# Layer 1's last two token blocks as a seven-product pair, in a kernel of chunked attention and two feed-forward layers

## The chip, the cores and the metric

One core of a Trainium2 chip. The metric is the device time of one execution in microseconds (us), lower is better. The engines are TensorE (PE; its weight loads are listed as PEld), VectorE (DVE), ScalarE (ACT), GpSimd (POOL) and SyncE (SP, which issues all DMAs of this kernel). Each engine works through its own instructions in the order in which the program issues them.

## The reference

```
scores = scale * q_c @ k_c^T            # 8 batches, 8 heads, 9 chunks of 64 tokens, head size 64
attn   = softmax(scores)
x      = attn @ v_c                     # as 4608 tokens x 512
x      = gelu_sigmoid(x @ w_in1) @ w_out1      # 512 -> 2048 -> 512
out    = prelu(x @ w_in2, alpha) @ w_out2      # 512 -> 2048 -> 512
```

Activations are fp32; the weights arrive as 64-bit floats and are decoded on the chip. Each operand of a feed-forward product is split into a high part, which TensorE's fp32r format holds, and the rest, and a product is the sum of three passes: high by high, low by high, high by low.

## The kernel before

Tokens go in 36 groups of 128 (`NG`), four to a block of 512 (`NB`, 9 blocks). The kernel has two stages.

**Stage 1** computes layer 1 block by block. A slot n is one block j and one of its 16 slices f of the hidden size: `emit_h` issues 12 matmuls for h = x w_in (three passes by four row tiles), Gelu on ACT, a copy to the high part on ACT and a subtraction for the low part on DVE (helper `split`, L123); `emit_y` issues 12 matmuls of y += g w_out, two slots behind: slot n issues h(n), then y(n-2). At the ends of a block this changes: slice 15 issues y(n-2) and y(n-1), slice 0 issues the last y of the block before, and slice 1 issues none. There are 144 slots. The sums y of a finished block are copied from PSUM and stored to DRAM (`x2d`). Slice 15 also splits the next block's x (`split_x`).

The attention of the groups and the preparation of layer 2's weights are put between these matmuls by a plan of half slots: half slot 2n is what `middle()` issues after h(n), and 2n+1 what follows y(n-2). A group g has these steps: `att_T` (q and k transposed by DVE, in blocks of 32), `att_S` (scores on PE, a row maximum and a subtraction on DVE: `att_S_max`), `att_X` (exponential on ACT, which loads another table first), `att_N` (three DVE instructions for the inverse of the row sum, then one multiplication on POOL), `att_AT` (eight DVE transposes), `att_PV` (32 matmuls, followed by the 32 score matmuls of the next group, then two ACT copies). From group 4 on a group starts every eight half slots (L1015): T at -5, X at -1, N at 0, AT at 2, PV at 5, the next group's S matmuls and maximum with PV. q and k are loaded by `load_qk` (L304): 32 DMAs of 16 KB for a group, in runs of 128 bytes, already in the order that `att_T` wants.

Layer 2 uses a scheme of seven products (Strassen-Winograd) for pairs of token blocks, so stage 1 also prepares the weights' combinations, in 32 steps (L1005), one per 3.25 slots from slot 18: load, absolute value on ACT, decode on DVE (four instructions), `prep_store_a` (ACT copy, POOL subtraction, four POOL sums) and `prep_store_b` (the same without sums). High and low parts go to DRAM (`wi2`, `wo2`). The store of a part is issued at once, and SP waits for it.

**Stage 2** (`second_layer`) works through five pairs (`PAIRS`, twice 512, 512, 512, 384, 384 tokens). A pair has four weight groups; a weight group is 14 h items of 6 matmuls and 7 y items of 12. A clock counts 1 for each h item and 2 for each y item. After an h pair ACT and DVE gather the product (`h_after`), apply the PReLU (`below`: three ACT instructions, `join`: one on DVE), and split the y operands (`op_hi` on ACT, `op_lo` on DVE); POOL forms four differences (L801). Weight tiles come from DRAM through two rings, reloaded after each use. While the last block of stage 1 runs, the first pair's x is loaded (`x_load`), its four sums formed on POOL (`x_sums`) and its seven operands split (`x_hi`, `x_lo`).

Of the kernel before, what the change touches and what calls it, by code (L numbers as in the profile page):

```python
# [32 lines left out]
PREP_FROM = 18  # L33
PREP_EVERY = 3.25

PAIRS = (512, 512, 512, 384, 384)
# [6 lines left out]
PLACE = {1: 0, 2: 1, 3: 6, 4: 2, 5: 3, 6: 4, 7: 5}  # L43

# [6 lines left out]
def tile_chunk_attention_two_ffn(  # L51
# [23 lines left out]
    NG = NT // P  # L75
    HP = H // 2
# [8 lines left out]
    gt_p = ctx.enter_context(tc.tile_pool(name="gt", bufs=2))  # L85
# [3 lines left out]

    first = ExitStack()  # L90
# [4 lines left out]
    prep_p = first.enter_context(tc.tile_pool(name="prep", bufs=1, reuse_waits="tile"))  # L95
# [12 lines left out]

    wi2 = [dram.tile([P, 7, 2, 2, P], F32, name=f"wi2_{j}") for j in range(NF // 2)]
# [114 lines left out]
    def prep_store(step, lo, hi, t):  # L224
        kind, j, m = step
        dst = wi2[j][:, lo:hi, m] if kind == "wi" else wo2[j // 2][:, lo:hi, j % 2, m]
        nc.sync.dma_start(
            out=dst.rearrange("p i a f -> p i (a f)"),
            in_=t.bitcast(F32).rearrange("p i a f -> p i (a f)"),
        )  # L230
# [11 lines left out]
    def prep_split(src, n, tag):  # L242
        t = prep_p.tile([P, n, 2, P], F32R, tag=tag, name=tag)
        nc.scalar.copy(t[:, :, 0], src)  # L244
        nc.gpsimd.tensor_tensor(out=t[:, :, 1], in0=src, in1=t[:, :, 0].bitcast(F32), op=ALU.subtract)  # L245
        return t

    def prep_store_a(step):
        u = pr[step]
        prep_store(step, 0, 3, prep_split(u[:, 0:3], 3, "sta"))  # L250
        sums = dec_p.tile([P, 4, P], F32, tag="u", name="sums")
        a11, a12, a22, a21 = (u[:, q] for q in range(4))
        for o, x, y, op in (
            (0, a21, a22, ALU.add), (1, sums[:, 0], a11, ALU.subtract),
            (2, a11, a21, ALU.subtract), (3, a12, sums[:, 1], ALU.subtract),
        ):
# [65 lines left out]

    qkT = {}

    def att_T(g):

        for nm in ("q", "k"):
            a = qkv.pop((g, nm))
            if g < GPB:
                t = spare(f"wo{NF - 3 - g % 2}", nm == "k").rearrange("p (h t) -> p h t", h=HP)  # L330
            else:
                t = qkt_p.tile([P, HP, P], F32, tag=nm + "T", name=nm + "T")
            if g < GPB + 2:
                ps = psum_att("psT")
                for hp in range(HP):
# [129 lines left out]
    def att_PV(g):  # L465
        at, vt = at_t.pop(g), qkv.pop((g, "v"))
        blk, i = divmod(g, GPB)
        if i == 0:
            x_t[blk] = x_p.tile([P, KT, NB], F32, tag="x", name="x")
# [27 lines left out]
    def split_x(j):  # L497
        if j not in x_t:
# [18 lines left out]
    gs_t = {}  # L517

    def emit_h(n, middle):
# [12 lines left out]
        g = gs[:, 0] if whole else gt_p.tile([P, NB], F32, tag="g", name="g")  # L532
        if f == NF - 1:
            split_x(j + 1)
        nc.scalar.activation(out=g, in_=ps, func=AF.Gelu_apprx_sigmoid)  # L535
        middle()
        if not whole:
            split(g, gs[:, 0], gs[:, 1], nc.scalar, nc.vector)
# [4 lines left out]
    def emit_y(n):  # L543
# [10 lines left out]
        if f == NF - 1:  # L554
            for t, ps in enumerate(y_t.pop(j)):
                if j == NBLK - 1:
                    sb = wpool.tile([P, 512], F32, tag=f"wo{8 + t}", name="ysb")
                else:
                    sb = dec_p.tile([P, 512], F32, tag="u", name="ysb")
# [10 lines left out]
    starts = [2 * sum(PAIRS[:p]) for p in range(NP)]  # L570
# [16 lines left out]
    def second_homes():  # L587
# [3 lines left out]
        for nm in ("b21", "b22", "t1", "t2", "t4"):  # L591
            homes[nm] = sec_p.tile([P, 1024], F32, tag=nm, name="x_" + nm)
        homes["wi2"] = []
        for k in range(2):
            t = sec_p.tile([P, 2, 2, 2, P], F32R, tag=f"wi2_{k}", name="wi2t")
            homes["wi2"] += [t[:, 0], t[:, 1]]
        for _ in range(4):
            load_wi()
# [20 lines left out]
    def x_load(p):  # L619
        n, t0 = PAIRS[p], starts[p]  # L620
        for half in range(2):
            for done, step, blk, s in x2_pieces(t0 + half * n, n):
                for c, names in ((0, ("b11", "b12")), (2, ("b21", "b22"))):
                    nc.sync.dma_start(
                        out=wide(homes[names[half]], n)[:, :, done:done + step],
                        in_=x2d[blk][:, c:c + 2, s:s + step],
# [44 lines left out]

    def load_wi():
        if wi_order:
# [4 lines left out]
            nc.sync.dma_start(out=t.bitcast(F32), in_=wi2[2 * gr + jj][:, PLACE[i]])  # L678
            wi_q.append(t)

    def load_wo():
        if wo_order:
# [4 lines left out]
            nc.sync.dma_start(out=t.bitcast(F32), in_=wo2[gr][:, PLACE[i]])  # L687
            wo_q.append(t)

    def second_layer():  # L690
# [12 lines left out]
        op_homes = [(home(f"op{k}h", F32R), home(f"op{k}l", F32R)) for k in range(4)]  # L703
# [7 lines left out]
        def at(when, fn, *args):  # L711
            due.setdefault(when, []).append((fn, args))

# [44 lines left out]
        def h_after(p, gr, i, jj):  # L758
# [6 lines left out]
            if jj == 0:  # L765
                return
            if i == 4:
# [7 lines left out]
            else:  # L775
# [3 lines left out]
                def rest():  # L779
                    neg = next_neg(n)  # L780
# [93 lines left out]
        def y_out(p, q):  # L874
# [3 lines left out]
            t = wide(homes[("b21", "b22", "t1", "t2")[q]], n)  # L878
            for d in range(2):
# [35 lines left out]
        while hs or ys:  # L915

            def y_next():
                nonlocal clock
                clock += 2
                if slot == nh or slot > nh + 1:  # L920
                    item = ys.pop(0)
                    y_item(*item)
                    load_wo()
                    y_after(*item)
# [7 lines left out]
            for _ in range(2 if hs else 0):  # L932
# [7 lines left out]
                load_wi()  # L940
                h_after(*item)
# [8 lines left out]
    with tc.manual_schedule():  # L950
# [53 lines left out]
        ]  # L1004
        for i, step in enumerate(steps):  # L1005
            n = PREP_FROM + int(i * PREP_EVERY)
            for what, lag, fn in (
                ("prep", 1, prep_load), ("abs", 3, prep_abs), ("prep", 3, prep_decode),
                ("prep", 4, prep_store_a), ("prep", 5, prep_store_b),
            ):  # L1010
                todo.setdefault((what, n + lag), []).append(partial(fn, step))


        between = {}
        for g in range(GPB, NG):  # L1015
            for at, fn in zip((-5, -1, 0, 2, 5), (att_T, att_X, att_N, att_AT, att_PV)):
                if g > GPB or at > 0:
                    when = 8 * (g - GPB) + at
                    between.setdefault(max(4, when) if fn is att_T else when, []).append((fn, g))
            if g + 1 < NG:  # L1020
                between.setdefault(8 * (g - GPB) + 6, []).append((load_v, g + 1))
            if g + 2 < NG:
                for part in range(8):
                    between.setdefault(max(0, 8 * (g - GPB) - 1 + part), []).append(
                        (partial(load_qk, part), g + 2)
                    )
# [3 lines left out]
        last_att = max(between) // 2  # L1030
        for n in range(NBLK * NF):
# [3 lines left out]

            def middle():
                nonlocal dec
                for fn, g in between.get(2 * n, []):
                    fn(g)
# [9 lines left out]
            for fn in todo.get(("abs", n), []):  # L1049
                fn()  # L1050


# [4 lines left out]
            for fn, g in between.get(2 * n + 1, []):  # L1057
                fn(g)
            for key in todo.get(("load", n), []):
                load_w(*key)  # L1060
            for fn in todo.get(("prep", n), []):
                fn()
            if n == NBLK * NF - NF + 2:
# [3 lines left out]
                second_homes()  # L1067
                x_load(0)
                for fn in x_sums(0):
                    fn()  # L1070
            if n >= NBLK * NF - 12 and n % 2 == 0:
                i = H_ORDER[(n - (NBLK * NF - 12)) // 2] if n < NBLK * NF - 0 else None
                x_hi(0, i)
                x_lo(0, i)
            if n == NBLK * NF - NF + 7:
                wo2_homes()
            if n == NBLK * NF - 3:
                more_homes()
        x_hi(0, H_ORDER[6])
        x_lo(0, H_ORDER[6])  # L1080
        emit_y(NBLK * NF - 1)
        banks.close()
        second_layer()


# [28 lines left out]
```

## Time and profile before

| | us |
|---|---|
| three runs | 1588.76, 1592.19, 3175.36 |
| their median | 1592.19 |
| the profiled execution | 1587.85 |
| its span on the core | 1586.0 |
| PE busy | 1560.1 (98%) |
| DVE, ACT, POOL busy | 1070.3, 835.8, 439.6 |

The span runs from the first to the last instruction on the core; the execution has 1.85 us around it. A busy PE is not PE at its peak, since matmuls are pipelined: the pace is read from how far apart runs of matmuls start.

### The profile page before, as it was taken

The page shows a single profiled execution, that of the slowest core. Times are in us where ns is not written, and L with a number is a line of the kernel's source. Part 1 is how long each engine was busy: PE and PEld are TensorE (multiplying, and loading weights), DVE is VectorE, ACT ScalarE, POOL GpSimd, SP SyncE. Part 2 cuts the span into 40 slices and gives each one's busy share as a digit, 9 for nine tenths or more (in the row PEclk, how much of TensorE's full clock was granted, in tenths as well). Part 3 has the DMA queues.
Part 4 walks back from the last instruction along what each step waited for, and adds up shares of the span by engine and source line. Part 5 has one row for each costly group of instructions (what it writes and reads, how often), then busy time and mean ns, then how long its engine had stood idle before and what let it go on. Part 6 is the DMA issues. An engine that isn't in the chain of part 4 may idle for free.

```text
span 1586.0 us, 25307 instructions
## 1 busy us (share of the span) xinstructions
PE 1560.1 (98%) x9309; PEld 1310.0 (83%) x9312; DVE 1070.3 (67%) x1442; ACT 835.8 (53%) x1198; POOL 439.6 (28%) x343
## 2 busy tenths in 40 slices
PE   7999999999999999999999999999999999999997
PEld 5678888888888888888888788888888888999997
DVE  6897656575666666566332477876887788688766
ACT  4665554454445545444333555665666556546653
POOL 3001322222222232222120235223422343352320
PEclk9999999999999999999999999999999999999999
DMA  9662445544444545444150676689668866997974
GB/s 247 189 170 59 95 106 145 122 130 115 128 114 115 133 124 135 123 116 116 37 199 1 184 226 214 188 216 280 192 191 218 267 187 213 243 335 233 279 256 120
DMA packets 384044, 268.08 MB, mean 169 GB/s; under 512 B 264112, under 2 KB 321968, under 8 KB 383920
## 3 DMA queue, kind: packets, MB, share of 16 engines
q1 hardware_dynamic: 383920, 266.46, 59.6%
q8 instruction: 74, 1.21, 0.3%
q14 instruction: 50, 0.41, 0.1%
HBM read 218.11 MB, written 48.23 MB: 168 GB/s over the span
## 4 chain that ended last, share of the span: by engine, by line
PE 93%; DVE 4%; ACT 2%; issue 1%; DMA 0%; DVEq 0%; ACTq 0%
PE psY L550 25%; PE psH L526 25%; PE psHa L731 12%; PE psYa L849 12%; PE psYb L849 9%; PE psHb L731 9%; PE psX L477 1%; PE psX L388 1%; DVE o L796 1%; ACT neg L748 0%; ACT neg L746 0%; DVE g L777 0%; DVE yacc L867 0%; DVE u L170 0%; PE warm L966 0%
## 5 line engine op out<-in xcount | busy, mean ns | idle before, releaser
L526 PE MATMUL psH<-xs,wi 128*128 128x512 f32 x1728 | 421.5, 394 | 1.1 <-ACT gs L535 1.1
L550 PE MATMUL psY<-gs,wo 128*128 128x512 f32 x1644 | 393.6, 389 | 0.0
L526 PEld LDWEIGHTS psH<-xs,wi 128*128 128x128 f32 x1728 | 322.9, 188 | 71.5 <-ACT gs L535 1.4
L550 PEld LDWEIGHTS psY<-gs,wo 128*128 128x128 f32 x1644 | 308.3, 188 | 64.1
L535 ACT ACTIVATE g<-psH 128x512 f32<-128x512 f32 x137 | 82.0, 599 | 307.1 <-PE psH L526 298.3
L128 DVE TENSOR_TENSOR gs<-g,gs 128x512 fp32r<-128x512 f32 x137 | 104.8, 765 | 202.3 <-ACT gs L125 201.9
L849 PE MATMUL psYa<-o,w 128*128 128x512 f32 (+1 forms) x960 | 212.0, 368 | 4.0 <-DVE o L796 2.1
L731 PE MATMUL psHa<-xop,wi2t 128*128 128x512 f32 (+1 forms) x960 | 211.1, 368 | 1.8 <-ACT g L769 1.4
L849 PEld LDWEIGHTS psYa<-o,w 128*128 128x128 f32 x960 | 175.0, 188 | 28.3 <-DVE o L796 3.8
L731 PEld LDWEIGHTS psHa<-xop,wi2t 128*128 128x128 f32 x960 | 175.3, 188 | 25.8 <-ACT g L769 1.8
L849 PE MATMUL psYb<-o,w 128*128 128x512 f32 (+1 forms) x720 | 158.4, 368 | 0.7 <-ACT o L791 0.7
L731 PE MATMUL psHb<-xop,wi2t 128*128 128x512 f32 (+1 forms) x720 | 158.1, 368 | 0.0
L849 PEld LDWEIGHTS psYb<-o,w 128*128 128x128 f32 x720 | 131.3, 188 | 18.4 <-ACT o L791 1.3
L746 ACT ACTIVATE neg<-g 128x1024 f32<-128x1024 f32 (+1 forms) x80 | 78.2, 977 | 128.9 <-DVE g L777 128.3
L801 POOL TENSOR_TENSOR tsum<-g,tsum 128x1024 f32<-128x1024 f32 (+1 forms) x39 | 100.7, 2583 | 163.2 <-DVE o L796 163.2
L731 PEld LDWEIGHTS psHb<-xop,wi2t 128*128 128x128 f32 x720 | 131.5, 188 | 17.4
L801 POOL TENSOR_TENSOR tsum<-g,g 128x1024 f32<-128x1024 f32 (+1 forms) x19 | 42.0, 2209 | 341.8 <-DVE g L754 341.8
L754 DVE SCALAR_TENSOR_TENSOR g<-g,neg 128x1024 f32<-128x1024 f32 (+1 forms) x80 | 104.4, 1305 | 15.8 <-ACT neg L748 15.8
L245 POOL TENSOR_TENSOR sta<-u,sta 128x384 fp32r<-128x384 f32 x32 | 33.4, 1045 | 259.8 <-ACT sta L244 229.6
L796 DVE TENSOR_TENSOR o<-tsum,o 128x1024 fp32r<-128x1024 f32 (+1 forms) x60 | 69.1, 1151 | 49.7 <-ACT o L791 49.6
L748 ACT ACTIVATE neg<-neg,minus_alpha 128x512 f32<-128x512 f32 (+1 forms) x160 | 100.4, 675 | 2.6
L796 DVE TENSOR_TENSOR o<-g,o 128x1024 fp32r<-128x1024 f32 (+1 forms) x60 | 96.9, 1614 | 4.9 <-ACT o L791 4.9
(131 smaller groups left out, 1796.7 us busy)
## 6 DMA issues: line engine op xcount, KB each, us to landing
wi2t<-wi SPq DMA_DIRECT2D x280, 256.0 KB, 3.7
w<-wo SPq DMA_DIRECT2D x140, 512.0 KB, 3.8
x<-ysb SPq DMA_DIRECT2D x36, 256.0 KB, 2.6
raw<-in_moe_w_in_dram SPq DMA_DIRECT2D x16, 512.0 KB, 5.0
raw<-in_moe_w_out_dram SPq DMA_DIRECT2D x16, 512.0 KB, 4.0
raw<-in_moe_w_in_dram SPq DMA_DIRECT2D x32, 256.0 KB, 4.0
wi<-stb SPq DMA_DIRECT2D x16, 512.0 KB, 3.3
raw<-in_moe_w_out_dram SPq DMA_DIRECT2D x32, 256.0 KB, 3.6
```

The source lines that it names most:

```text
L128: eng_lo.tensor_tensor(out=lo, in0=src, in1=hi.bitcast(F32), op=ALU.subtract)
L245: nc.gpsimd.tensor_tensor(out=t[:, :, 1], in0=src, in1=t[:, :, 0].bitcast(F32), op=ALU.subtract)
L526: nc.tensor.matmul(ps, w[:, a, c], xs[:, b, c], start=(i == 0), stop=(i == 3 * KT - 1))
L535: nc.scalar.activation(out=g, in_=ps, func=AF.Gelu_apprx_sigmoid)
L550: nc.tensor.matmul(y_t[j][t], w[:, a, t * P:(t + 1) * P], gs[:, b], start=(f == 0 and a + b == 0), stop=(f == NF - 1 and b == 1),)
L731: nc.tensor.matmul(ps, w[:, c, a], x[b][:, c], start=(k == 0 and i in (1, 2, 5)), stop=(k == 5 and i in (2, 3, 4)), skip_group_check=True,)
L746: nc.scalar.activation(out=neg, in_=src, func=AF.Relu, scale=-1.0)
L748: nc.scalar.activation(out=neg[:, jj], in_=neg[:, jj], func=AF.Copy, scale=minus_alpha[:, f + jj:f + jj + 1])
L754: nc.vector.scalar_tensor_tensor(out=g, in0=g, scalar=0.0, in1=neg, op0=ALU.max, op1=ALU.add)
L796: nc.vector.tensor_tensor(out=lo, in0=wide(homes[nm], n), in1=hi.bitcast(F32), op=ALU.subtract)
L801: eng.tensor_tensor(out=wide(homes[out], n), in0=wide(homes[x], n), in1=wide(homes[y], n), op=ALU.subtract,)
L849: nc.tensor.matmul(ps[:, d, :n], w[:, jj, d, a], x[b][:, jj], start=(k == 0 and i in (1, 5, 2)), stop=(k == 5 and i in (3, 2, 4)), skip_gr ...
```

## The change

The last two blocks (7 and 8, groups 28 to 35) leave stage 1's slots, of which 112 are left (`NPL` = 7 blocks), and become a first pair of stage 2 (`PAIRS_1`) with layer 1's weights. Their attention output goes to DRAM (`x1d`). The pair has the same items as layer 2's, with Gelu where those have the PReLU, and its output goes to `x2d` without a transpose. Its weight combinations are made by a new POOL step `fold`, 32 times, one per 4.7 half slots from half slot 40: two additions of 128x256 (the high and low part of decoded weights) and four of 128x128; they are stored as fp32, and each weight tile is split when it has been loaded (`split_factor`: ACT copy; subtraction on POOL for w_in tiles of 128x256, on DVE for w_out tiles of 128x512).

All 32 groups must be done within 112 slots. From the fifth on they follow at six half slots, in the order `GROUP_ORDER`, the i-th at half slot base = 32 + 6(i-4). q and k of groups from 8 on are first copied from DRAM to DRAM (`sort_qk`, eight DMAs of 512 runs of 128 bytes for a group), then loaded as two whole tiles (`load_sorted`); `att_T` then writes every fourth column. The preparation's step i has b = 36 + int(5.5 i): load at half slot b, absolute value b+3, decode b+4, store_a b+6, store_b b+8. Within a half slot the plan lists attention first, then preparation and fold in the order of i. Stores of prepared tiles are issued two half slots later (`send_later`). The high part of g is copied before `middle()` instead of after it, from block 1 on. The diff, cut to its core:

```diff
-PREP_FROM = 18
-PREP_EVERY = 3.25
-PAIRS = (512, 512, 512, 384, 384)
+PREP_FROM = 36
+PREP_EVERY = 5.5
+FOLD_FROM = 40
+FOLD_EVERY = 4.7
+PAIRS_1 = (512,)
+PAIRS_2 = (512, 512, 512, 384, 384)
+PAIRS = PAIRS_1 + PAIRS_2
+GROUP_ORDER = (
+    4, 5, 6, 7, 8, 9, 10, 11, 28, 29, 12, 13, 14, 15, 30, 16, 17, 18, 19, 31,
+    20, 21, 22, 23, 32, 33, 24, 25, 26, 27, 34, 35,
+)
...
     def prep_store_a(step):
+        a11, a12, a22, a21 = (pr[step][:, q] for q in range(4))
+        sums = dec_p.tile([P, 4, P], F32, tag="u", name="sums")
+        quarter_sums(a11, a12, a21, a22, *(sums[:, o] for o in range(4)))
+        prep_store(step, 0, 3, prep_split(pr[step][:, 0:3], 3, "sta"))
...
+    def fold(step):
+        kind, j, m = step
+        u = prep_p.tile([P, 7, P], F32, tag="fold", name="fold")
+        for k in range(2):
...
+            nc.gpsimd.tensor_tensor(out=o, in0=t[:, 0], in1=t[:, 1], op=ALU.add)
+        a11, a12, a21, a22, s0, s1, s2 = (u[:, o] for o in range(7))
+        quarter_sums(a11, a12, a21, a22, s0, s1, s2, a21)
...
+    def sort_qk(part, g):
...
+            nc.sync.dma_start(
+                out=qk_d[g, nm][part % 4, off:off + n],
+                in_=src[b, par::2, s:s + n, y * SQ:(y + 1) * SQ].rearrange("h t e -> t h e"),
+            )
...
+            else:
+                nc.vector.transpose(
+                    t.rearrange("p h (t b) -> p b h t", b=4),
+                    a.rearrange("p (b h e) -> p b h e", b=4, h=HP),
                 )
...
         nc.scalar.activation(out=g, in_=ps, func=AF.Gelu_apprx_sigmoid)
+        early_hi = j > 0
+        if early_hi:
+            nc.scalar.copy(gs[:, 0], g)
         middle()
...
+    def split_factor(hi, lo, eng):
+        nc.scalar.copy(hi, lo.bitcast(F32))
+        eng.tensor_tensor(out=lo, in0=lo.bitcast(F32), in1=hi.bitcast(F32), op=ALU.subtract)
...
+        def split_soon():
+            while unsplit:
+                at(clock + 3, split_factor, *unsplit.pop(0))
...
+            if i == 4 and p < N1:
+                nc.scalar.activation(out=g("21"), in_=src, func=AF.Gelu_apprx_sigmoid)
+                return
...
+                    if p < N1:
+                        nc.scalar.activation(out=g(nm), in_=g(nm), func=AF.Gelu_apprx_sigmoid)
+                        return
...
-        for g in range(GPB, NG):
-            for at, fn in zip((-5, -1, 0, 2, 5), (att_T, att_X, att_N, att_AT, att_PV)):
+        for i, g in enumerate(GROUP_ORDER):
+            if i < GPB:
+                times = ((att_T, -5), (att_X, -1), (att_N, 0), (att_AT, 2), (att_PV, 5))
+            else:
+                times = ((att_T, -5), (att_S_max, -1), (att_X, 0), (att_N, 1), (att_AT, 2), (att_PV, 4))
...
-        for n in range(NBLK * NF):
+        for n in range(NPL * NF):
```

## Rows read from the trace of the kernel before

**Rows 1.** The page: busy shares (part 1), and PE's granted clock in slices (part 2).
```profile
PE 1560.1 (98%) x9309; PEld 1310.0 (83%) x9312; DVE 1070.3 (67%) x1442; ACT 835.8 (53%) x1198; POOL 439.6 (28%) x343
...
PEclk9999999999999999999999999999999999999999
```

**Rows 2.** Waits of PE: engine line, what it waited for; us, times, longest.
```profile
PE psS L359 <- ACT early L341: 2.5, 3, 1.1
PE psYa L849 <- DVE o L796: 2.1, 3, 1.1
```

**Rows 3.** By stretch: us, busy PE, PEld, DVE, ACT, POOL, PEclk, DMA, GB/s.
```profile
370.00:490.00 120.00, 120.00 (x822) 98.65 (x821) 73.27 (x134) 56.73 (x90) 32.18 (x42) 1.00 0.48 121
...
1027.50:1180.20 152.70, 152.70 (x674) 126.16 (x673) 120.49 (x99) 90.84 (x104) 55.62 (x21) 1.00 0.76 220
```

**Rows 4.** Chain that ended last, in order of time: start, us, piece (452 to 473 us).
```profile
452.77 0.62 PE psX L477 x32
...
459.54 2.72 PE psH L526 x12
...
464.98 2.72 PE psH L526 x12
```

**Rows 5.** Timeline of one group's attention steps in stage 1: start us, us, engine, line.
```profile
456.85 0.60 ACT L535 ACTIVATE g<-psH 128x512 f32<-128x512 f32 x1 [1.86 <-PE psH L526]
...
458.13 1.28 ACT L408 ACT_TABLE_LOAD   x1
...
459.42 0.63 ACT L408 ACTIVATE e<-e 128x512 f32<-128x512 f32 x1
...
460.09 0.69 DVE L413 TENSOR_REDUCE d<-e 128x8 f32<-128x512 f32 x1 [1.25 <-ACT e L408]
...
460.64 1.31 POOL L245 TENSOR_TENSOR stb<-sums,stb 128x512 fp32r<-128x512 f32 x1 [2.75 <-ACT stb L244]
...
460.81 1.18 DVE L414 TENSOR_SCALAR d<-d 128x8 f32<-128x8 f32 x1
...
462.30 1.04 POOL L416 TENSOR_TENSOR e<-e,d 128x512 f32<-128x512 f32 x1 [0.34 <-DVE d L415]
...
464.19 3.60 DVE L448 STREAM_TRANSPOSE at<-e 32x256 f32<-32x256 f32 x8
...
464.68 6.03 SPq L318 DMA_DIRECT2D q<-in_q_dram  x12
...
475.78 0.69 PE L477 MATMUL psX<-at,v 64*64 64x64 f32 x32
```

**Rows 6.** One line's instructions, duration ns min/median/max: the addition in `att_N`.
```profile
L414 DVE TENSOR_SCALAR d<-d x36: 171/174/1175, 11.7 to 761.0; 128x8 f32<-128x8 f32 x36
```

**Rows 7.** Groups by shape: instructions and operation, tiles, count | busy us, mean ns.
```profile
L343 DVE STREAM_TRANSPOSE qT<-q 128x512 f32<-128x512 f32 x30 | 21.1, 703 | 0.0
...
L170 DVE SCALAR_TENSOR_TENSOR u<-raw,u 128x512 int32<-128x512 int32 x64 | 43.0, 689 | 1.3
...
L160 DVE TENSOR_SCALAR u<-u 128x512 f32<-128x512 f32 x64 | 28.0, 455 | 3.6 <-ACT u L157 3.6
...
L245 POOL TENSOR_TENSOR sta<-u,sta 128x384 fp32r<-128x384 f32 x32 | 33.4, 1045 | 259.8 <-ACT sta L244 229.6 <-DMA k<-in_k_dram 30.1
...
L257 POOL TENSOR_TENSOR sums<-u,sums 128x128 f32<-128x128 f32 x32 | 15.2, 476 | 0.0
...
L128 DVE TENSOR_TENSOR gs<-g,gs 128x512 fp32r<-128x512 f32 x137 | 104.8, 765 | 202.3 <-ACT gs L125 201.9
```

**Rows 8.** Groups by shape, ACT and DVE instructions that the pair's steps use.
```profile
L746 ACT ACTIVATE neg<-g 128x1024 f32<-128x1024 f32 x48 | 51.0, 1063 | 82.2 <-DVE g L777 81.8
...
L748 ACT ACTIVATE neg<-neg,minus_alpha 128x512 f32<-128x512 f32 x96 | 64.4, 718 | 1.6
...
L487 ACT COPY x<-psX 128x256 f32<-128x256 f32 x72 | 23.2, 376 | 68.1 <-PE psX L388 63.4 <-PE psX L477 4.6
...
L754 DVE SCALAR_TENSOR_TENSOR g<-g,neg 128x1024 f32<-128x1024 f32 x48 | 72.4, 1508 | 12.3 <-ACT neg L748 12.3
```

More of the change, by code (lines that the diff above doesn't have):

```diff
@@ L106, in tile_chunk_attention_two_ffn @@
     x2d = [dram.tile([P, KT, NB], F32, name=f"x2_{j}") for j in range(NBLK)]
+    x1d = {j: dram.tile([P, KT, NB], F32, name=f"x1_{j}") for j in range(NPL, NBLK)}
+    wi1 = [dram.tile([P, 7, 2, P], F32, name=f"wi1_{j}") for j in range(NF // 2)]
+    wo1 = [dram.tile([P, 7, 2, 2, P], F32, name=f"wo1_{g}") for g in range(NF // 4)]
     wi2 = [dram.tile([P, 7, 2, 2, P], F32, name=f"wi2_{j}") for j in range(NF // 2)]
@@ L222, in prep_load, with send_later, send_due, prep_store @@
         pr[step] = decode_raw([raw.rearrange("p q f -> p (q f)")])
-    def prep_store(step, lo, hi, t):
+    waiting = []
+    half = 0
+    def send_later(**dma):
+        waiting.append((half + 2, dma))
+    def send_due():
+        while waiting and waiting[0][0] <= half:
+            nc.sync.dma_start(**waiting.pop(0)[1])
+    def prep_store(step, lo, hi, ts):
         kind, j, m = step
         dst = wi2[j][:, lo:hi, m] if kind == "wi" else wo2[j // 2][:, lo:hi, j % 2, m]
[L227 to L230, printed above, removed]
+        for a, t in enumerate(ts):
+            send_later(out=dst[:, :, a], in_=t)
     def prep_abs(step):
@@ L569, in tile_chunk_attention_two_ffn @@
     NP = len(PAIRS)
-    starts = [2 * sum(PAIRS[:p]) for p in range(NP)]
+    starts = [
+        NPL * NB + 2 * sum(PAIRS_1[:p]) if p < N1 else 2 * sum(PAIRS_2[:p - N1]) for p in range(NP)
+    ]
     NJ = NF // 2
@@ L702, in second_layer @@
         home("t3")
-        op_homes = [(home(f"op{k}h", F32R), home(f"op{k}l", F32R)) for k in range(4)]
+        op_homes = [(home(f"op{k}h", F32R), home(f"op{k}l", F32R)) for k in range(3)]
+        op_homes.append((
+            prep_p.tile([P, 1024], F32R, tag="raw2", name="op3h"),
+            gt_p.tile([P, 1024], F32R, tag="g", name="op3l"),
+        ))
         yacc = x_p.tile([P, 4, 2, max(PAIRS)], F32, tag="xs", name="yacc")
@@ L1004, in tile_chunk_attention_two_ffn, with base @@
         ]
+        between = {}
+        def base(i):
+            return 8 * i if i < GPB else 8 * GPB + 6 * (i - GPB)
+        for i, g in enumerate(GROUP_ORDER):
+            if i < GPB:
+                times = ((att_T, -5), (att_X, -1), (att_N, 0), (att_AT, 2), (att_PV, 5))
+            else:
+                times = ((att_T, -5), (att_S_max, -1), (att_X, 0), (att_N, 1), (att_AT, 2), (att_PV, 4))
+            for fn, at in times:
+                if g > GPB or at > 0:
+                    when = base(i) + at
+                    between.setdefault(max(4, when) if fn is att_T else when, []).append((fn, g))
+            if i + 1 < len(GROUP_ORDER):
+                between.setdefault(base(i) + 6, []).append((load_v, GROUP_ORDER[i + 1]))
+            if g >= QK_DRAM:
+                for part in range(8):
+                    when = base(i) - 24 + part * 6 // 8
+                    between.setdefault(when, []).append((partial(sort_qk, part), g))
+                between.setdefault(base(i) - 12, []).append((load_sorted, g))
+            elif g >= GPB + 2:
+                for part in range(8):
+                    when = max(0, base(i - 2) - 1 + part)
+                    between.setdefault(when, []).append((partial(load_qk, part), g))
@@ L1005, in tile_chunk_attention_two_ffn @@
         for i, step in enumerate(steps):
[L1006 to L1009, printed above, removed]
-            ):
-                todo.setdefault((what, n + lag), []).append(partial(fn, step))
-        between = {}
-        for g in range(GPB, NG):
-            for at, fn in zip((-5, -1, 0, 2, 5), (att_T, att_X, att_N, att_AT, att_PV)):
[L1017 to L1026, printed above, removed]
+            b = PREP_FROM + int(i * PREP_EVERY)
@@ L1028, in tile_chunk_attention_two_ffn @@
+            for when, fn in (
+                (b, prep_load), (b + 3, prep_abs), (b + 4, prep_decode), (b + 6, prep_store_a),
+                (b + 8, prep_store_b), (FOLD_FROM + int(i * FOLD_EVERY), fold),
+            ):
+                between.setdefault(when, []).append((fn, step))
         dec = decode_w(todo.get(("decode", 0), []))
         next(dec)
-        last_att = max(between) // 2
-        for n in range(NBLK * NF):
+        for n in range(NPL * NF):
             blk, f = divmod(n, NF)
@@ L1034, in tile_chunk_attention_two_ffn, with half_slot @@
                 split_whole(f)
+            def half_slot(k):
+                nonlocal half
+                half = k
+                send_due()
+                for fn, x in between.pop(k, []):
+                    fn(x)
             def middle():
                 nonlocal dec
-                for fn, g in between.get(2 * n, []):
-                    fn(g)
+                half_slot(2 * n)
                 for key in list(dec_t):
@@ L1070, in tile_chunk_attention_two_ffn @@
                     fn()
[L1071 to L1075, printed above, removed]
+            if 2 <= to_go <= 8:
+                x_hi(0, H_ORDER[8 - to_go])
+                x_lo(0, H_ORDER[8 - to_go])
+            if to_go == 6:
                 wo2_homes()
-            if n == NBLK * NF - 3:
+            if to_go in (8, 3):
+                while unsplit:
+                    split_factor(*unsplit.pop(0))
+            if to_go == 2:
                 more_homes()
-        x_hi(0, H_ORDER[6])
-        x_lo(0, H_ORDER[6])
-        emit_y(NBLK * NF - 1)
+        assert not between
+        emit_y(NPL * NF - 1)
         banks.close()
+        while unsplit:
+            split_factor(*unsplit.pop(0))
         second_layer()
```

144 lines of the change are left out of this document (99 added, 45 removed).

## The prediction

> **What bounds the kernel now.** I read the page first, then the waits, then the time by stretch, the chain in order of time and the timeline of one attention group. The page shows PE busy for 1560 of 1586 us at the full granted clock [rows 1]; the longest waits of PE on anyone are 2.5 and 2.1 us in all [rows 2]. In stage 1 and in a whole pair of stage 2, PE is busy for all of the stretch, while DVE has 61% and 79%, ACT 47% and 59%, POOL 27% and 36% [rows 3]. So the time is PE's stream of matmuls, and what the other engines do is free as long as PE never waits. The pace: two runs of h lie 464.98 - 459.54 = 5.44 us apart, with the 12 matmuls of y between them, so 24 matmuls take 5.44 us and one takes 0.2267 us [rows 4]. A whole pair takes 152.7 us for 4 x 168 = 672 matmuls, the same 0.227 [rows 3]. An attention group comes every 23.0 us (PV at 452.77 and at 475.78) [rows 4, 5], which is four slots and 1.25 us of its own matmuls.
>
> The view that decides is the timeline of a group [rows 5], since its steps are what the change moves closer together. From the Gelu of the slot (456.85) it shows: table load at 1.28, exponential ending at 3.20 us, DVE's row sum at 3.24, POOL's multiplication at 5.45, eight DVE transposes from 7.34 to 10.94, and PV only at 18.93. Eight us of slack, so nothing in this chain costs time now.
>
> **What the change takes away.** Two blocks are 2 x 16 x 24 = 768 matmuls of stage 1; the pair that replaces them has 672 of the same width. 96 x 0.2267 = **21.8 us less**. That is 1.4% of the time, while a measurement of this kernel tells about 2% from no change: a clear gain can't come from this, and the question is what is given back. The attention's matmuls stay the same in number.
>
> **Load of stage 1.** A group now gets 3 x 5.44 + 1.25 = 17.6 us in place of 23.0. In the 120 us of stage 1 shown, DVE has 73.3 us, of which about 15.9 are the low parts of g (20.8 slots at 0.765 [rows 7]); the other 57.4 grow at most by 23.0/17.6 = 1.31, to 75, so DVE is at 91 of 120. ACT by the same step comes to about 66. POOL comes to 32 x 1.31 = 42, and to the folds: a fold is two additions of 128x256, between 0.48 (128x128) and 1.05 (128x384), taken halfway at 0.76, and four of 0.48, in all 3.4 us [rows 7]; one in 4.7 half slots (13.8 us) makes 30, together 72 of 120. No engine is full, so what counts is order and lateness.
>
> **The attention chain.** Now X is at base, N at base+1, AT at base+2, PV at base+4. X stands behind the Gelu and high part of an even half slot, as in the rows, so the start of the chain is as shown: exponential done 3.2 us after the Gelu of slot base/2. PV follows the h of two slots later: 2 x 5.44 = **10.9 us** after that Gelu, in place of 18.9. The chain in its new order: N takes 1.2 us up to POOL's start when its addition runs at the median 0.17 [rows 6] (in the timeline it took 1.18, and ended with POOL's subtraction at 461.95 [rows 5]). Then `att_T` of the next group, now in the same half slot as N, takes two transposes, 1.4 us [rows 7], beside POOL's 1.04. Then AT, 3.6. So 3.2 + 1.2 + 1.4 + 3.6 = 9.4 us, 1.5 us before PE asks. The normal group still costs nothing, but the cover is gone for all that comes on top. PE waits directly at PV, and y and h queue behind it. From the plan:
>
> - *POOL late.* Groups 10, 18 and 26 have, in the half slot of base, store_b, then a fold; group 32 has store_a, then a fold. POOL takes them in order before N's multiplication. The subtraction waits for an ACT copy behind the exponential, so it starts at about 3.8 and ends at 5.1 (1.31 [rows 5]); the fold ends at 8.5, the multiplication at 9.6, AT at 13.2: 2.3 us late, three times. With store_a (1.05 [rows 7]) 2.0. In all 9.0. If the fold ran before the subtraction it would cost nothing, but the list has it behind.
> - *Decode late.* Groups 11, 19 and 27 have a decode at base+1 between T and AT: two instructions of 0.46 and two of 0.69 [rows 7], 2.3 us. AT ends at 11.7: 0.8 us late, in all 2.4.
> - *Short windows.* Where base is slice 0 or 1 of a block, one y run lies elsewhere, and PV comes after 8.2 us. Group 16: 1.2 us late; 35 (no T behind it) 0.9; groups 8 and 20, at slice 0, have two more DVE copies of finished y ahead of N: 2.1 each. In all 6.3.
>
> Together 17.7 us. The bounds: 0, if all queues run further ahead than I read, and about 34, if T costs twice as much (below) and every such group is 0.4 us later.
>
> **The rest of stage 1.** A DMA of 128 short runs takes SP 0.5 us (12 in 6.03) [rows 5]; 32 for a group are 16 us of 23. The eight sorting DMAs have four times the runs: from 0.5 us each (4 us) to four times that (16 us), I take 1 us, 8 us a group. SP is not on the path either way; at the upper end it would fill 16 of 17.6 us and loads could come late. The DMA engines' 0.48 [rows 3] becomes at most 0.48 x 1.31 plus the sorted loads. Transfers have 12 half slots (33 us) before the load: no cost.
>
> **The pair.** Per weight group of 38.2 us, from a quarter of the pair's row [rows 3]: ACT has 22.7; it loses four PReLUs of 1.06 + 2 x 0.72 = 2.5, gains three Gelus of about 1.0 (the fourth replaces a copy), 14 copies of about 0.38 and 7 of 0.62 (about the Gelu's 0.60 for this shape [rows 5]) [rows 8]: 25.3. DVE has 30.1; minus four joins of 1.51 [rows 8], plus seven subtractions of 0.77 [rows 7]: 29.5. POOL has 13.9, plus 14 subtractions of about 0.76: 24.5. All fit, and Gelu's chain is shorter than the PReLU's. What is new is that ACT's copy waits for a DMA; it stands three clocks behind, 4.1 us or more. I take **1 us** for the seam and the pair, between 0 and 8 (half a us of lateness in four h or y items of each weight group).
>
> **Sum.** 1587.9 (the profiled execution) - 21.8 + 17.7 + 1 = **1585 us**. The median of the three runs is 4 us above the profiled execution, the lower run 1 us; I leave that in the range.
>
> **The rivals.**
> A. *The gain is kept* (0.28). The late steps do not reach PE, because POOL and DVE start them earlier than I place them. For it: DVE and POOL have 24% and 40% idle time left, and the present plan shows no wait at all. Against it: in all four POOL cases an ACT copy behind the exponential stands ahead of the fold. Lateness of 0 to 7 us: 1566 to 1574, taken as 1570.
> B. *The strided transposes* (0.2): the other side, slower than before. `att_T` now writes every fourth fp32, 16 bytes apart; every DVE transpose in the trace writes runs of at least 32 elements, so no row prices it. Its price lies between the 1.4 us of the two transposes and twice that, nearest to the row: I take 1.4. If it is twice, then after N each chain is 1.4 longer: decode and short windows with a T cost 6 x 1.4 = 8.4 more, the five groups with a subtraction alone ahead (14, 15, 17, 23, 25) 0.5 to 1.0 each, 3.7 in all, the POOL cases nothing. 1585 + 12 = 1597. It decides above about 1.9 us for the two: 0.5 us more in those six eat the 3 us that remain of the gain.
> [...]
> C. *The pair does not run at PE's pace* (0.07). Where POOL works, DVE stretches (the addition, 0.17 to 1.18 [rows 6]), and POOL's share in the pair rises from 36% to 64%. If DVE's 29.5 grew by a third to 39, each of the four weight groups would take 1 us or more longer, and late splits would add PE waits: 5 to 20 us, 1590 to 1605. Against it: DVE already works beside POOL in the row that I took.
> D. *The plan breaks down* (0.03): a queue blocks (SP behind the sorting, ACT behind a store), and stage 1 stalls in every group by 2 us or more: 28 x 2 = 56, above 1620.
>
> **How the numbers follow.** My own case, 1578 to 1592, has 0.42. With A at its left and B and C at its right the range is **1567 to 1605**. Faster by over 2% (below 1560) would need more than PE gives up: 0.02. Slower by over 2% (above 1624) needs D or several others together: 0.04. Within 2%: 0.94.
>
> **What would show it.** Right: the chain has about 24 x 112 matmuls in stage 1 and 672 at 0.227 in the first pair, 21.8 us less of PE's busy time; PE's waits name the matmuls of `att_PV`, waiting for DVE's transposes of `at`, ten or so of 1 to 2.5 us, near 18 us in all, the longest in groups 10, 18, 26 with POOL's multiplication behind a fold. T at 0.70 us keeps my sum; T at 1.2 or more proves B. Wrong: no waits at PV (A), waits in the first pair (C), or waits of PE on Gelu or on DMA.

## The result, and the profile after

Measured: 1604.47 us (median of four runs, 1602.5 to 1606.2) against 1590.97 before; the ratio is **1.0089**, 95% interval 1.0068 to 1.0110. The ratio leaves out the run of before that took 3175.36 us; the other three have a median of 1589.75. The change makes the kernel 0.9% slower, where I had forecast 1585 us and a small gain. The profiled execution took 1603.7 us, its span 1601.9. From the page of the changed kernel, parts 1 and 2, which answer to [rows 1]:

```profile
PE 1553.7 (97%) x9213; PEld 1300.1 (81%) x9216; DVE 1179.9 (74%) x1496; ACT 889.2 (56%) x1278; POOL 669.5 (42%) x611
...
PEclk9999999999999999999999999999999999999999
```

PE has 96 matmuls less, but is busy for only 6.4 us less than before, not 21.8, and it is idle for 48 us in place of 26. So both terms are visible at once: PE waits more, and what it does takes longer. (The clock's digits don't show it: 9 stands for 90% or more.) The waits of PE in the changed kernel, which answer to [rows 2]:

```profile
PE psX L557 <- DVE at L524: 19.9, 15, 1.8
PE psX L407 <- ACT qT L412: 3.5, 1, 3.5
PE psYa L974 <- DVE o L921: 2.8, 4, 1.0
```

The first line is `att_PV` waiting for DVE's transposes of `at`: near the 18 us forecast, in the form forecast. That is not all that was lost. I split the difference by the starts of the h runs. Up to slot 18 both kernels agree within 0.2 us. From there to the first pair the time before is 727.55 us; 32 slots of 5.44 less would leave 553.5; measured are 585.4, so stage 1 loses **31.9 us**. From the first pair to the end there are 158.2 us more, where one more whole pair would take 152.7 [rows 3]: **5.5 us** more. Together -174.1 + 152.7 + 31.9 + 5.5 = 16.0, and the span grew by 15.9.

Group 10 shows how a wait of 3.3 us becomes a loss of 5.2. From the timeline of the changed kernel (start us, us, engine, line; the idle time before it in brackets), to be set beside [rows 5]:

```profile
176.22 0.60 ACT L621 ACTIVATE g<-psH 128x512 f32<-128x512 f32 x1 [3.38 <-PE psH L612]
...
178.78 0.63 ACT L484 ACTIVATE e<-e 128x512 f32<-128x512 f32 x1
...
180.00 1.30 POOL L271 TENSOR_TENSOR sums<-sums,stb 128x512 fp32r<-128x512 f32 x1 [4.27 <-ACT stb L269]
180.16 1.15 DVE L490 TENSOR_SCALAR d<-d 128x8 f32<-128x8 f32 x1
...
181.24 1.47 POOL L304 TENSOR_TENSOR fold<-wi 128x256 f32<-128x256 f32 x2
...
181.47 1.06 DVE L419 STREAM_TRANSPOSE qT<-q 128x512 f32<-128x512 f32 x1
...
182.38 1.09 DVE L419 STREAM_TRANSPOSE kT<-k 128x512 f32<-128x512 f32 x1
...
182.78 2.73 POOL L279 TENSOR_TENSOR fold<-fold 128x128 f32<-128x128 f32 x4
183.30 0.42 DVE L176 TENSOR_SCALAR u<-u 128x512 f32<-128x512 f32 x1
...
184.18 2.88 PE L612 MATMUL psH<-xs,wi 128*128 128x512 f32 x12
...
185.22 0.83 DVE L191 SCALAR_TENSOR_TENSOR u<-raw,u 128x512 int32<-128x512 int32 x1
185.47 1.49 POOL L492 TENSOR_TENSOR e<-e,d 128x512 f32<-128x512 f32 x1
...
186.99 3.60 DVE L524 STREAM_TRANSPOSE at<-e 32x256 f32<-32x256 f32 x8 [0.94 <-POOL e L492]
...
188.82 0.33 PE L557 MATMUL psX<-at,v 64*64 64x64 f32 x4 [1.76 <-DVE at L524]
...
190.65 0.62 PE L557 MATMUL psX<-at,v 64*64 64x64 f32 x26 [1.50 <-DVE at L524]
...
191.73 4.62 PE L641 MATMUL psY<-gs,wo 128*128 128x512 f32 x12
...
196.18 1.08 PE L612 MATMUL psH<-xs,wi 128*128 128x512 f32 x4
```

POOL does the subtraction, then the fold to 185.5, then N's multiplication to 186.96; DVE has meanwhile finished T and the decode at 186.05. AT ends at 190.6, and PE, which asked at 187.06, stands for 1.76 us, does four matmuls, and stands for 1.50 more. Then comes what I had not priced: the next 12 matmuls of y take 4.62 us in place of the 2.88 of a run of 12. The granted clock over these 20 us is below 1 (by stretch: us, busy PE, PEld, DVE, ACT, POOL, PEclk, DMA, GB/s):

```profile
180.00:200.00 20.00, 16.74 (x125) 13.38 (x124) 12.31 (x21) 7.76 (x14) 15.13 (x21) 0.91 0.79 204
380.00:400.00 20.00, 16.74 (x120) 13.52 (x119) 13.30 (x22) 9.05 (x15) 12.18 (x17) 0.83 0.94 247
```

By shorter stretches of the same trace, the granted clock was 1.00 from 186 to 191 us, through both waits of PE, 0.50 from 192 to 195, and 1.00 again from 196 to 199. The second row is group 18, where it was 1.00 from 387 to 393 us and 0.50 from 394 to 400. From one h start to the next, slot 24 takes 196.18 - 184.18 = 12.0 us; a slot with PV and S takes 459.54 - 452.77 = 6.77 [rows 4]. So group 10 costs 5.2 (the same group costs 3.6 where the granted clock stays up: e4 and e6 below).

### The profile page after: what moved, and what is told of

Read it like the earlier page. It is cut to its first block, busy times and chain, and to the rows that moved or that the text cites. A ratio compares the mean times of both kernels' runs of the same rounds, so it can differ in the third digit from the quotient of the medians.

```text
span 1601.9 us, 25268 instructions
## 1 busy us (share of the span) xinstructions
PE 1553.7 (97%) x9213; PEld 1300.1 (81%) x9216; DVE 1179.9 (74%) x1496; ACT 889.2 (56%) x1278; POOL 669.5 (42%) x611
## 4 chain that ended last, share of the span: by engine, by line
PE 80%; DVE 7%; POOL 3%; DMA 3%; ACT 3%; issue 2%; SPq 1%; POOLq 0%; DVEq 0%; ACTq 0%
PE psY L641 15%; PE psYa L974 14%; PE psHa L850 14%; PE psH L612 13%; PE psYb L974 10%; PE psHb L850 10%; DVE at L524 2%; DMA raw<-in_moe_w_in_dram 1%; PE psX L557 1%; PE psX L464 1%; DMA v<-in_v_dram 1%; ACT L484 1%; DVE o L921 1%; SPq L365 1%; DVE d L489 1%
## 5 line engine op out<-in xcount | busy, mean ns | idle before, releaser
L612 PE MATMUL psH<-xs,wi 128*128 128x512 f32 x1344 | 324.8, 391 | 1.1 <-ACT gs L621 1.1
L641 PE MATMUL psY<-gs,wo 128*128 128x512 f32 x1260 | 311.5, 398 | 0.0
L612 PEld LDWEIGHTS psH<-xs,wi 128*128 128x128 f32 x1344 | 251.7, 188 | 55.6 <-ACT gs L621 1.6
L641 PEld LDWEIGHTS psY<-gs,wo 128*128 128x128 f32 x1260 | 238.8, 191 | 51.4
L926 POOL TENSOR_TENSOR tsum<-g,tsum 128x1024 f32<-128x1024 f32 (+1 forms) x47 | 124.0, 2638 | 182.5 <-DVE o L921 150.8
L850 PE MATMUL psHa<-xop,wi2t 128*128 128x512 f32 (+1 forms) x852 | 190.6, 372 | 0.4 <-DVE g L899 0.4
L974 PEld LDWEIGHTS psYa<-o,w 128*128 128x128 f32 x864 | 159.0, 189 | 31.5 <-DVE o L921 4.9
L926 POOL TENSOR_TENSOR tsum<-g,g 128x1024 f32<-128x1024 f32 (+1 forms) x23 | 52.1, 2265 | 291.8 <-DVE g L873 272.8
L629 DVE TENSOR_TENSOR gs<-g,gs 128x512 fp32r<-128x512 f32 x105 | 81.5, 787 | 100.1 <-ACT gs L624 98.7
L492 POOL TENSOR_TENSOR e<-e,d 128x512 f32<-128x512 f32 x32 | 35.3, 1103 | 188.1 <-DVE d L491 155.7
L524 DVE STREAM_TRANSPOSE at<-e 32x256 f32<-32x256 f32 x224 | 97.1, 433 | 9.9 <-POOL e L492 6.8
L994 DVE TENSOR_TENSOR yacc<-psYb,yacc 128x1024 f32<-128x1024 f32 (+1 forms) x64 | 72.2, 1128 | 41.8 <-PE psYb L974 41.5
```

Source lines behind the costliest of these rows:

```text
L524: nc.vector.transpose(t3[o * SQ:(o + 1) * SQ, :, i % 2 * SQ:(i % 2 + 1) * SQ], e[i * SQ:(i + 1) * SQ, :, b * SQ:(b + 1) * SQ],)
L612: nc.tensor.matmul(ps, w[:, a, c], xs[:, b, c], start=(i == 0), stop=(i == 3 * KT - 1))
L629: nc.vector.tensor_tensor(out=gs[:, 1], in0=g, in1=gs[:, 0].bitcast(F32), op=ALU.subtract)
L641: nc.tensor.matmul(y_t[j][t], w[:, a, t * P:(t + 1) * P], gs[:, b], start=(f == 0 and a + b == 0), stop=(f == NF - 1 and b == 1),)
L850: nc.tensor.matmul(ps, w[:, c, a], x[b][:, c], start=(k == 0 and i in (1, 2, 5)), stop=(k == 5 and i in (2, 3, 4)), skip_group_check=True,)
L926: eng.tensor_tensor(out=wide(homes[out], n), in0=wide(homes[x], n), in1=wide(homes[y], n), op=ALU.subtract,)
```

## The experiments

For each kernel this is the lateness of the slots that hold a group's PV, in us, worked out in this way from the starts of h (5.44 for a plain slot, 2.72 at slice 1, 8.16 at slice 15, 1.32 for PV and S); a dash is under 0.3.

| group | late by, as forecast | after | e1 | e2 | e3 | e4 | e5 | e6 | e7 | e8 |
|---|---|---|---|---|---|---|---|---|---|---|
| 10 | POOL 2.3 | 5.2 | 3.0 | 2.4 | 0.8 | 3.6 | 4.9 | 3.6 | 1.0 | 0.3 |
| 18 | POOL 2.3 | 6.5 | 3.7 | 4.0 | - | 3.6 | 4.9 | 5.2 | - | - |
| 26 | POOL 2.3 | 5.2 | 3.7 | 4.0 | - | 3.6 | 4.9 | 5.1 | - | - |
| 32 | POOL 2.0 | 3.7 | - | 2.1 | - | 2.4 | 3.6 | 2.1 | - | - |
| 11 | decode 0.8 | 1.8 | 1.8 | - | - | 3.4 | 1.5 | 1.8 | - | - |
| 19, 27 | decode 0.8 each | 1.2, 1.2 | 1.2, 1.2 | - | - | 1.2, 1.2 | 0.5, 0.5 | 1.2, 1.2 | - | - |
| 8, 20 | window 2.1 each | 1.9, 1.9 | 3.5, 1.9 | 1.9, 1.9 | 3.5, 1.9 | 1.9, 1.9 | 1.4, 1.4 | 3.5, 3.5 | 1.9, 1.9 | - |
| 16, 35 | window 1.2, 0.9 | 1.7, 0.7 | 1.6, 0.7 | 1.7, 0.7 | 1.7, 0.7 | 1.6, 0.7 | 1.2, 0.7 | 1.6, 0.7 | 1.7, 0.7 | - |
| 28, 34 | - | - | - | 0.5, 2.2 | 1.2, 4.0 | - | - | - | 0.9, 1.4 | 0.5, 0.5 |
| 30 | - | 0.5 | 0.4 | 1.0 | 1.0 | 1.0 | 0.3 | 1.0 | 1.0 | 0.3 |
| 12, 17, 21 | - | - | 0.3, -, - | - | 0.4, -, - | - | - | - | - | 0.7, 0.8, 0.6 |
| all of stage 1 from slot 18 | 17.7 | 31.6 | 23.2 | 22.5 | 15.2 | 26.4 | 26.1 | 30.8 | 10.5 | 3.2 |

Each column is one execution, and e6 shows how far a cell can be trusted: its edit is in the pair alone, so its stage 1 is that of the change. Yet groups 8, 10, 18, 20 and 32 differ by 1.3 to 1.6 us between the two columns, and the granted clock differs with them. Around group 8, first in the changed kernel, then in e6 (by stretch, as above):

```profile
145.00:165.00 20.00, 18.50 (x140) 15.02 (x139) 13.31 (x25) 13.76 (x22) 5.50 (x5) 1.00 0.62 158
145.00:165.00 20.00, 18.50 (x132) 14.85 (x131) 11.77 (x21) 12.21 (x19) 3.57 (x3) 0.91 0.62 158
```

PE waits 1.5 us ahead of this group's PV in both, and the 12 matmuls of y behind it take 3.0 us in one and 4.6 in the other. So a difference of some 1.5 us in one cell is no effect of an edit by itself. Nor do the medians of four runs tell all: the intervals of e4, e5 and e6 overlap that of the change, and what these three show is read from their traces.

**e1: folds one half slot earlier.**

```diff
+                if fn is fold and when in bases:
+                    when -= 1
```

> Changed kernel 1604.5 us; only the six folds that share the half slot of a group's X are issued one half slot earlier. Theory M (two late things at once): in groups 10, 18 and 26 POOL's multiplication behind the fold ends only about 1 us after DVE's decode, so without the fold the decode still makes PE wait: 1 us less in each (up to 2.8 where PE's clock then stays up); group 32, which has no decode, loses all of its 3.7 us. 1592 to 1599. Rival L (load): the waits come from DVE and POOL being fuller in general, so they only move to other groups: within 3 us of 1604.

Measured: 1596.1 us, ratio to before 1.0045 (1.0025 to 1.0066). Group 32 is free; 10, 18 and 26 keep 3.0 to 3.7.

**e2: decodes two half slots later.**

```diff
+                if fn is prep_decode and when - 1 in bases:
+                    when += 2
```

> Only the six decodes that stand between N and AT are issued two half slots later. M: groups 11, 19 and 27 lose their waits (4.2 us in all); in 10, 18 and 26 the multiplication behind the fold stays late, 1.3 us earlier than now (3 where the clock then stays up); group 32 stays at 3.7. 1591 to 1597. L: within 3 us of 1604.

Measured: 1596.7 us, ratio 1.0049 (1.0034 to 1.0065). Groups 11, 19 and 27 are free, 10, 18, 26 and 32 keep 2.1 to 4.0; group 34 is new, with 2.2.

**e3: both edits.**

> Both edits. M: groups 10, 11, 18, 19, 26, 27 and 32 go from 24.8 us of lateness to under 2: 1580 to 1583, which is more than the gains of the two single edits together. Where lateness simply adds (rival A), the gain is the sum of the two. L: within 3 us of 1604.

Measured: 1586.1 us, ratio 0.9982 (0.9970 to 0.9995). The single edits gain 8.4 and 7.8 us, both together 18.3; the 2.2 us above the sum are no more than the noise of these medians, but the table shows why there should be some: in groups 10, 18 and 26 the multiplication behind the fold and the decode end within 1 us of each other, and while one stays, most of the wait stays. Load (L) falls: the same work on the same engines costs PE half. The seven groups of these edits go from 24.8 to 0.8 us, as expected. The expected 1580 to 1583 was missed all the same, since groups 28 and 34 are now late, by 1.2 and 4.0 us. (The traced execution took 1590.3 us, 4 above the median; the clock fell in it behind groups 8 and 34.) The timeline of e3 at group 34, and the stretch behind it:

```profile
609.34 0.66 ACT L173 ACTIVATE u<-raw 128x512 f32<-128x512 f32 x1 [1.37 <-DMA raw<-in_moe_w_out_dram]
...
612.25 0.83 DVE L191 SCALAR_TENSOR_TENSOR u<-raw,u 128x512 int32<-128x512 int32 x1
...
614.71 0.67 DVE L489 TENSOR_REDUCE d<-e 128x8 f32<-128x512 f32 x1
...
618.50 3.84 DVE L590 TENSOR_TENSOR xs<-x,xs 128x512 fp32r<-128x512 f32 x4
...
622.27 3.59 DVE L524 STREAM_TRANSPOSE at<-e 32x256 f32<-32x256 f32 x8
```

```profile
620.00:640.00 20.00, 17.88 (x131) 14.54 (x130) 13.56 (x26) 9.62 (x16) 3.69 (x4) 0.91 0.48 148
```

ACT waits for a load of the preparation that could start only after the moved decode (one buffer), DVE's next decode comes late, N (L489) behind it, and `split_x` (L590) then stands before AT. A moved step took its queue with it.

**e4: PE kept busy in the four POOL waits.**

```diff
+        for _ in range(22 if g in (10, 18, 26, 32) else 0):
+            nc.tensor.matmul(
+                ps[0][:, :HP * CH], ident.bitcast(BF16)[:, :P], ident.bitcast(BF16), start=True, stop=True
+            )
```

> The changed kernel with 22 small matmuls ahead of PV in groups 10, 18, 26 and 32 alone, into the place that PV then overwrites: PE works where it now waits. The late transposes stay. Theory C (the granted clock falls because PE stood idle): the four runs of y behind these waits go back from about 4.5 to 2.7 us, granted clock 1.00 there, 6 to 8 us less: 1597 to 1599. Rival (those runs are slow for another reason, such as operands or DMA): no gain, 1604 to 1607.

Measured: 1599.4 us, ratio 1.0067 (1.0050 to 1.0085). By stretch:

```profile
180.00:200.00 20.00, 19.09 (x154) 15.67 (x153) 13.25 (x22) 9.37 (x16) 15.15 (x21) 1.00 0.76 192
380.00:400.00 20.00, 19.09 (x154) 15.64 (x153) 13.30 (x22) 9.60 (x15) 12.24 (x17) 1.00 0.92 228
```

The granted clock is 1.00 in both stretches, against 0.91 and 0.83 in the change, the y run behind group 10 spreads its starts over 2.7 us again, and the four groups lose 13.4 in place of 20.6 us: 7.2 less, as theory C says. The matmuls added are of no use to the result and the late transposes stay, so the gain is the clock's. It isn't one lucky execution: the change, e5 and e6 have these four waits too, and in ten of their twelve the granted clock over the 20 us around was between 0.83 and 0.93, in e4 in none of four. How much is lost differs: the four groups lose 20.6 us in the change, 18.4 in e5 and 16.0 in e6. In e4 one fall turned up behind group 11 (3.4 us late in place of 1.8); the traced execution gains 4.7 us in all, the median 5.0, which is 0.4 short of the range expected.

**e5: `att_T` writes runs of 32.**

```diff
-                    t.rearrange("p h (t b) -> p b h t", b=4),
+                    t.rearrange("p h (b t) -> p b h t", b=4),
```

> The changed kernel with one access pattern changed: att_T writes runs of 32 elements in place of every fourth, from the same loads (so tokens within a group are in another order, and the attention computed is another one; work and sizes are the same). Theory: the two transposes go from 1.97 back to about 1.35 us, and where T stands in the last chain (groups 8, 11, 16, 19, 20, 27) PE waits 0.6 us less each; the four POOL groups stay. 1599 to 1602. Rival (T's length is hidden or was always 1.97): 1603 to 1606.

Measured: 1600.6 us, ratio 1.0077 (1.0060 to 1.0094). One line's instructions (duration ns min/median/max), first in the changed kernel, then in e5:

```profile
L419 DVE STREAM_TRANSPOSE qT<-q x28: 1041/1054/1107, 127.4 to 632.7; 128x512 f32<-128x512 f32 x28
L419 DVE STREAM_TRANSPOSE kT<-k x28: 1062/1076/1099, 128.3 to 633.6; 128x512 f32<-128x512 f32 x28
```

```profile
L419 DVE STREAM_TRANSPOSE qT<-q x28: 659/660/705, 129.0 to 629.7; 128x512 f32<-128x512 f32 x28
L419 DVE STREAM_TRANSPOSE kT<-k x28: 668/670/671, 129.6 to 630.3; 128x512 f32<-128x512 f32 x28
```

Only the stride differs, and it makes each transpose 0.4 us longer (the two take 2.13 us in the change, not the 1.97 that the expectation has). The groups late by decode or window gain 0.3 to 0.7 each, except 35, which has no T behind it.

**e6: the pair's sums early.**

```diff
-            at(u + 62, x_load, p + 1)
+            at(u + (34 if p < N1 else 62), x_load, p + 1)
...
-                at(u + 76 + 3 * k, fn)
+                at(u + (48 + 8 * k if p < N1 else 76 + 3 * k), fn)
```

> The changed kernel; in the first pair alone the next pair's x is loaded 28 clocks earlier and its four POOL sums are issued at 48, 56, 64 and 72 in place of 76 to 85. Theory P (the pair's loss is one pile-up on POOL, four sums of 3.4 us among the weight splits, behind which ACT and PE wait near 846 us): the pair goes from 158.5 to about 153.5 us, the granted clock stays 1.00 there: 1598 to 1601. Rival (the pair is slower throughout, through DVE or the split copies): 1603 to 1606.

Measured: 1598.6 us, ratio 1.0067 (1.0047 to 1.0086). From the first pair's first h to the next pair's, the changed kernel takes 139.4 us (the first pair before: 135.3), e6 135.1. In the changed kernel's timeline the pile-up ends so (with the stretch behind it):

```profile
836.23 2.85 POOL L728 TENSOR_TENSOR t<-x_b,x_t 128x1024 f32<-128x1024 f32 x1
...
839.04 3.39 POOL L926 TENSOR_TENSOR t<-g,g 128x1024 f32<-128x1024 f32 x1
...
842.39 2.39 POOL L926 TENSOR_TENSOR tsum<-g,tsum 128x1024 f32<-128x1024 f32 x1
...
844.82 1.04 ACT L916 CAST o<-tsum 128x1024 fp32r<-128x1024 f32 x1 [5.77 <-POOL tsum L926]
...
845.92 0.49 PE L974 MATMUL psYa<-o,w 128*128 128x512 f32 x1 [1.22 <-ACT o L916]
```

```profile
846.00:852.00 6.00, 5.12 (x15) 3.87 (x16) 6.00 (x4) 4.42 (x8) 5.91 (x5) 0.72 0.13 41
```

The last x sum (L728) and the differences (L926) come one behind the other, ACT waits 5.8 us for the second, PE for ACT, and 11 of its 12 matmuls there run late and for the most part at a granted clock of 0.50 (847.4 to 850.7 us; 0.72 over these 6 us). The low clock isn't what makes the loss: in e2 the clock stays at 1.00 here, PE waits 4.2 us in this pair in place of 2.8, and the pair takes 139.5. One place, not a slow pair: theory P holds.

**e7: decodes directly behind AT** (as e3, with `when += 1`).

> As e3_both, but the six decodes stand directly behind the transposes of AT (one half slot later than in the change, not two), so the next raw load, which waits for the decode, starts earlier. Theory: in e3 the new waits of groups 28 and 34 (1.2 and 4.0 us) come from that late load (ACT stood on it); they go, others stay: 1580 to 1584. Rival (they come from DVE alone): 1585 to 1588.

Measured: 1586.3 us, ratio 0.9985 (0.9974 to 0.9996), no gain over e3 by the median, and inside the rival's range. In the profiled execution groups 28 and 34 lose 0.9 and 1.4 us in place of 1.2 and 4.0. Part of the 4.0 is the clock's: in e2, with the decode as late and the clock at 1.00, group 34 loses 2.2. So the late load is at most a part of their cause, and how much is not settled.

**e8: all mended** (e7 and e6, and these):

```diff
-                times = ((att_T, -5), (att_S_max, -1), ... (att_AT, 2), (att_PV, 4))
+                times = ((att_T, -5 if i == GPB else -7), (att_S_max, -1), ...
+                         (att_AT, 2), (att_PV, 4 + (base(i) // 2 % NF < 2)))
```

> e7, with att_T two half slots earlier (out of the chain), PV one half slot later where the window is short (groups 8, 16, 20, 35), and the pair's sums early as in e6. If the step list is right, hardly a wait of the 31.6 us in stage 1 is left (under 4), and the pair runs at 153.5: 1568 to 1574, which is faster than both kernels. If load is what counts, waits stay and it is above 1578.

Measured: **1572.9 us**, ratio 0.990 (0.9885 to 0.9915): faster than both kernels, 31.5 us below the change. Its stretches at the same places:

```profile
180.00:200.00 20.00, 20.00 (x147) 16.36 (x146) 12.94 (x25) 12.54 (x21) 13.52 (x18) 1.00 0.74 190
380.00:400.00 20.00, 20.00 (x148) 16.34 (x146) 15.12 (x30) 8.99 (x14) 9.51 (x13) 1.00 0.76 197
```

PE has no gap and a granted clock of 1.00 at both places. Of 21.8 us of fewer matmuls 15.7 reach the time against the runs of before beside it (1588.6).

## Why the prediction was wrong, step by step

Two views that the list draws on: a stretch of stage 1 of the changed kernel (as above), and POOL's fold and multiplication of group 10 in e2, where the decode no longer stands beside them.

```profile
387.00:507.00 120.00, 114.35 (x896) 93.23 (x895) 90.66 (x154) 58.91 (x94) 69.83 (x100) 0.97 0.77 200
```

```profile
180.74 1.47 POOL L304 TENSOR_TENSOR fold<-wi 128x256 f32<-128x256 f32 x2
...
182.29 1.96 POOL L279 TENSOR_TENSOR fold<-fold 128x128 f32<-128x128 f32 x4
184.21 1.05 POOL L492 TENSOR_TENSOR e<-e,d 128x512 f32<-128x512 f32 x1
```

- *What is taken away* held: the same pace of matmuls, 96 fewer; e8 collects most of it.
- *The load of stage 1* held: I had DVE at 91 and POOL at 72 of 120 us, and the changed kernel shows 90.7 and 69.8. e3, with the same load and half of the lateness, shows that load isn't the cause. A sorting DMA took SP 0.63 us at the median, where I had taken 1, and no wait of PE names a DMA.
- *The attention chain* was the right place, and the eleven groups named are the eleven that lose 0.7 us or more. The failed step is the term **POOL late**: 9.0 us forecast, 20.6 measured. Two things were mis-sized in it. First, in groups 10, 18 and 26 the fold took 4.2 us (1.47 + 2.73), not 3.4, and the multiplication 1.49, not 1.04, both beside DVE's decode: these groups have a decode at base+1 as well, and I had counted it in 11, 19 and 27 alone. In e2, with the decode moved away, the same work takes 3.4 and 1.05, and group 10 is late by 2.4 at a granted clock of 1.00, against 2.3 forecast; with the decode it is 3.6 (e4, e6). Group 32, which has no decode, is late by 2.1 in e6, against 2.0. The four together lose 13.4 in e4, not 9.0. Second, I priced a wait at its own length. In the changed kernel the granted clock fell behind it (to 0.50 from 192 to 195 us in group 10, from 394 to 400 in group 18), and the 12 matmuls of y there took 4.62 and 5.05 us in place of 2.88; against e4 this is 7.2 us over the four groups in the change, and under 3 in e6. No row of before could show that price, since in the stage 1 shown there PE is busy for all of the stretch [rows 3], but the bounds for an unseen wait should have had room for it.
- *Decode late*: 2.4 forecast, 4.2 measured, by T's stride (e5: 0.3 to 0.7 a group). Rival B's effect was real, at little over half of its price (0.8 us for the two transposes, against 1.4): T takes 2.1 us, above the 1.9 from which I let it decide, and a transpose lies between the 0.70 and the 1.2 us that I had named as signs. The measured price, 1.05 to 1.08 against 0.66 to 0.67 us, is 1.6 times. No row or run shows the double that rival B took, and the bound of 34 us with it; it was an assumption.
- *Short windows*: 6.3 forecast, 6.2 measured, in part by luck: e5, with the transposes near their former length, has 4.8 there, and e6, where the clock falls behind groups 8 and 20, has 9.3.
- *The pair*: 1 forecast (0 to 8), 5.5 measured. Of this 4.0 is in the first pair. I compared averages ("All fit"), and the average held (POOL has 97.9 us in the pair, 24.5 a weight group forecast), while POOL was busy for 29.6 of the 30 us from 820 to 850, around the x sums, which I had spread over the whole pair; e6 takes back 4.2. The rest is in the three full pairs behind it: each takes 153.25 us, where before it took 152.65, in e8 too. No run says why.
- *Sum*: the errors are 11.6 + 1.8 + 4.5, and 0.8 in the small waits; 1587.9 - 21.8 + 31.9 + 5.5 gives 1603.5, and the execution took 1603.7. I had given 0.28 to rival A, for which nothing came, and rivals C and D did not occur as described. That the time lies inside 1567 to 1605 is luck: my own case ended at 1592, the room above it was made for B and C, and most of the error is neither.

## What to carry to other kernels

Where a step chain is moved closer to its consumer, follow each queue in program order for the worst coincidence of the plan, not the average load: here eleven of 28 groups cost nearly everything in stage 1, and a half slot for six folds and six decodes gave back 18 us. Two late things that end together must both be moved, or neither edit shows all of its worth. And here the waits of TensorE cost more than their length where the granted clock fell behind them (7.2 us over four groups, against e4), so a wait of some us that was not there before is to be priced with room for slow matmuls behind it.

## What the runs showed of the hardware that I had not expected

- After waits of 1.76 and 1.50 us in a row the granted clock showed 0.91 over 20 us (0.50 from 192 to 195 us), and twelve matmuls took 4.62 us in place of 2.88; with useless matmuls in the wait it stayed at 1.00 (e4). The fall did not come each time: with the same instructions and the same wait of 1.5 us ahead of group 8's PV, the clock was 1.00 over the 20 us around in the changed kernel and 0.91 in e6, and likewise 0.91 in e1 and e3.
- DVE's strided transpose took 1.05 to 1.08 us against 0.66 to 0.67 in e5: 1.6 times, above.
- DVE and POOL took longer beside each other, both ways. The addition on 128x8, 0.17 us at the median of the changed kernel, took 1.15 us beside POOL's subtraction and ended with it (181.30); POOL's four additions took 2.73 us beside DVE's decode, where they took 1.96 in e2 with the decode moved away. All eleven additions of the changed kernel that took over 0.3 us, this one among them, ended within 0.03 us of a POOL instruction.
